# VectorE's SBUF-only steps and GpSimd's additions in turns, long-row copies of two weights in DRAM, and a new schedule table

## The chip, the core and the metric

The kernel runs on one core of a Trainium2 chip. The metric is the device time of one execution in microseconds. It is compared as the median of several runs; the kernel before has a median of 1410.25 us over 3 runs (1404.16 to 1413.4).

Five engines work side by side, each through its own queue of instructions in a fixed order: TensorE (PE, matrix products), ScalarE (ACT, here the exponentials), VectorE (DVE), GpSimd (POOL) and SyncE (SP, which issues transfers). They wait for each other by semaphores.

## The reference

Two transformer-like blocks are applied twice to x of 2048 rows and 512 columns, all in bfloat16:

```python
def _A_ref(x, wqkv, wo):                      # 32 heads of 16
    q, k, v = split(x @ wqkv)
    scores = einsum("bhqd,bhkd->bhqk", q, k) * (Dh ** -0.5)
    p = softmax(scores)
    return reshape(einsum("bhqk,bhkd->bhqd", p, v)) @ wo
def _B_ref(x, w1, w2):                        # 512 -> 1792 -> 512
    return maximum(x @ w1, 0) @ w2
x = x + _A_ref(_layernorm(x), wqkv, wo)
x = x + _B_ref(_layernorm(x), w1, w2)
x = x + _A_ref(_layernorm(x), wqkv, wo)
x = x + _B_ref(_layernorm(x), w1, w2)
```

Each attention has 32 x 2048 x 2048 scores, and each score needs an exponential. That is most of the work.

## The kernel before

**A planner writes the order.** The kernel's text is a planner: it keeps a clock for each engine (`now_pe`, `now_dve`, `now_pool`, `now_act`), adds a cost for every step it emits, and emits the next step that it believes to be ready. The result is a fixed order of instructions per engine. The costs are constants at the head (L78 to L91), such as `POOL_ADD`, the cost of one GpSimd addition, and `JOINING`, the cost of issuing one joining transfer (below). `STARTS`, `MORE`, `SLIP` and `RULES` (L96, L105) are tables of exceptions to the planner's rules, keyed by the number of the slot.

**Slots.** Scores are made in blocks of 128 keys by 512 queries. The main loop (L2066) takes three blocks in a turn, called a slot; there are 1365 slots. TensorE writes the three blocks into one of two PSUM tiles `ps_s` (L2231). ScalarE then takes the exponential of two or of all three of them in one instruction (L2249: 128x1024 or 128x1536).

**Pairs.** Where ScalarE takes two blocks, VectorE takes the third. Two such blocks, of two slots, make a *pair*. Their exponential is an approximation in integer words: VectorE turns the scores into 16-bit words (`first_step`, L1750: from PSUM to a buffer of `words`), GpSimd makes two shifted copies of the words with 64-bit integer additions (`shifted`, L1811: `up` and `down`, one instruction each for both blocks), and the copies enter the value product with weights. Where the keys have no copy of the values that is already scaled, VectorE scales `down` in place (`weigh`, L1816, SBUF to SBUF). Buffers for words are borrowed from whatever lies idle (x rows, weights, values), so the profile shows the same lines with many names.

**Joining.** Unjoined, a pair gives three products with the values. If the pair is *joined* (`joins`, L1795), GpSimd issues a transfer that adds the unshifted words onto `up` (`add`, L1829, 256 KB, done by the DMA engines), and two products are left. The issue is an instruction (DMA_DIRECT2D, L1830) in GpSimd's own queue, between its additions, and counts as busy time of GpSimd. In `chain` (L1800), the joining task is given a delay of 300 ns after its `up` (`late`), and an addition's result counts as made `BEHIND_IT` = 300 ns after the addition.

**Value products.** TensorE multiplies the exponentials and the words with the values (`pv`, L1404), four heads abreast, into `ps_o` or `ps_f`. Between scores and values it fits the other matrix products (L467, L707, L716): projections, output and the dense block.

**VectorE's other steps.** Most read PSUM. These read and write SBUF alone: `ln_apply` (L795, 60 times, the layer norm's second half), `weigh` (L1816), `scale_v` (L945, 12 times), `mul` (L1342, 43 times, the division by the softmax sum). Each stands in VectorE's queue where the planner put it.

**Weights.** W1 does not stay in SBUF. It streams through four buffers: `load_w1` (L1025) issues, on SP, one load for each 128 columns, straight from the input, four groups ahead; a row of such a load is 256 bytes. `w1_to_load` (L1064) loads ten more such pieces late in the run. `load_w2` (L1649) fetches pairs of 128-row pieces of w2 again after their place has served as words. `to_load` (L274) lists the first loads of wo and w2; from slot 30 on the main loop issues one a slot (L2299), the last six from slot 180 on.

Of the kernel before, what the change touches and what calls it, by code (L numbers as in the profile page):

```python
# [12 lines left out]
BF16 = mybir.dt.bfloat16  # L13
# [13 lines left out]
def kernel(  # L27
# [11 lines left out]
    P = 128  # L39
# [38 lines left out]
    POOL_ADD = 170.0 + 215.0 * GROUP  # L78
# [12 lines left out]
    JOINING, ADDED, BEHIND_IT = 870.0, 4300.0, 300.0  # L91
# [4 lines left out]
    STARTS, MORE, SLIP = {13: 0, 90: 1, 113: 1, 120: 1, 109: 1, 101: 1, 127: 1, 188: 1, 194: 1, 193: 0, 218: 1, 207: 0, 256: 0, 260: 0, 286: 1, 292: 0, 313: 0, 329: 1, 322: 1, 323: 0, 336: 1, 353: 0, 360: 0, 373: 0, 374: 0, 385: 0, 439: 0, 442: 1, 502: 1, 516: 0, 532: 0, 530: 0, 585: 1, 605: 0, 653: 0, 641: 0, 655: 0, 678: 1, 694: 0, 684: 0, 689: 1, 692: 0, 770: 0, 776: 1, 818: 1, 807: 1, 808: 0, 806: 0, 822: 0, 852: 1, 842: 0, 879: 0, 880: 0, 916: 0, 937: 0, 941: 1, 948: 0, 952: 1, 950: 1, 962: 1, 961: 0, 983: 0, 1015: 1, 1011: 1, 1003: 0, 1017: 1, 1021: 1, 1027: 1, 1026: 1, 1022: 1, 1056: 0, 1058: 1, 1044: 0, 1055: 0, 1076: 1, 1092: 0, 1108: 0, 1128: 1, 1139: 0, 1130: 1, 1131: 0, 1151: 1, 1150: 0, 1155: 0, 1146: 0, 1227: 0, 1235: 0, 1256: 1, 1285: 0, 1352: 0}, {18: 1.0, 12: 1.0, 87: 2.0, 107: 1.0, 103: -1.0, 119: 2.0, 126: 1.0, 158: 1.0, 181: 2.0, 201: 2.0, 233: -1.0, 238: 1.0, 240: 1.0, 242: 2.0, 245: 1.0, 258: 2.0, 264: 2.0, 265: -1.0, 266: 1.0, 300: 2.0, 308: 1.0, 320: 2.0, 318: -1.0, 348: 1.0, 361: -1.0, 395: -1.0, 412: 1.0, 401: 1.0, 402: 2.0, 422: 2.0, 426: 2.0, 439: 1.0, 441: -1.0, 452: -1.0, 453: 1.0, 465: 2.0, 500: -1.0, 507: 1.0, 515: 2.0, 531: 1.0, 536: -1.0, 533: 1.0, 560: 2.0, 574: 2.0, 580: 2.0, 575: -1.0, 589: -1.0, 631: -1.0, 645: -1.0, 666: -1.0, 675: -1.0, 680: 2.0, 767: 1.0, 762: 1.0, 770: 2.0, 813: 1.0, 811: 2.0, 802: 2.0, 827: 2.0, 855: -1.0, 841: 1.0, 847: 1.0, 868: -1.0, 874: -1.0, 878: 1.0, 884: -1.0, 908: -1.0, 927: 1.0, 942: 1.0, 945: -1.0, 959: 1.0, 965: 1.0, 997: -1.0, 1017: 2.0, 1046: 1.0, 1089: 1.0, 1100: -1.0, 1099: -1.0, 1158: -1.0, 1176: 2.0, 1234: 1.0, 1223: 1.0, 1222: 2.0, 1258: -1.0, 1326: -1.0, 1332: -1.0, 1331: -1.0, 1356: 2.0, 1347: 2.0, 1360: 2.0, 1362: 1.0, 1374: 1.0}, {88: -200.0, 133: -200.0, 175: -200.0, 184: -200.0, 227: 60.0, 367: 120.0, 366: 60.0, 364: 120.0, 418: 60.0, 401: 216.0, 415: 120.0, 445: 120.0, 451: 120.0, 459: 120.0, 463: 60.0, 482: 60.0, 519: 216.0, 518: 216.0, 515: 216.0, 549: 120.0, 572: 60.0, 574: 216.0, 568: 216.0, 592: 216.0, 589: 216.0, 594: 60.0, 621: 120.0, 652: 216.0, 646: 120.0, 642: 60.0, 663: -200.0, 697: 216.0, 682: 60.0, 754: 60.0, 746: 216.0, 742: -200.0, 771: 216.0, 817: 60.0, 809: 216.0, 802: 60.0, 850: -200.0, 848: 60.0, 859: 120.0, 909: 60.0, 916: 60.0, 902: 120.0, 935: -200.0, 974: 120.0, 992: -200.0, 996: 120.0, 1025: -200.0, 1064: 120.0, 1068: -200.0, 1097: 60.0, 1116: -200.0, 1169: 120.0, 1220: -200.0, 1218: 60.0, 1232: 216.0, 1234: -200.0, 1230: 60.0, 1256: 216.0, 1268: -200.0, 1264: 120.0, 1273: 120.0, 1332: 120.0, 1336: -200.0, 1340: 216.0, 1353: -200.0, 1347: 120.0, 1354: 120.0, 1376: 60.0}  # L96
# [8 lines left out]
    RULES = {1: {'young': 6, 'old': 4, 'slack': 1300.0, 'ahead': 1.0, 'haste': 1.3, 'fill': 4000.0, 'partial': 3, 'hold': 4}, 21: {'fill': 3000.0, 'join': 4000.0}, 81: {'cap': 3.0, 'hold': 2, 'join': 1500.0, 'over': 60.0, 'near': 6, 'far': 4, 'spare': 14, 'wide': 1}, 101: {'near': 8}, 121: {'near': 8, 'pressed': 2, 'soon': 1400.0, 'old': 4}, 141: {'wide': 0, 'closing': 9}, 161: {'pressed': 6, 'hold': 3, 'spare': 6, 'least': 0.8, 'far': 4, 'soon': 2000.0, 'haste': 1.6, 'near': 4}, 201: {'margin': 60.0, 'spare': 10, 'backlog': 2200.0, 'young': 6, 'far': 2, 'least': 0.5, 'hold': 2, 'slack': 1300.0}, 221: {'calm': 2.0, 'closing': 12, 'soon': 2000.0, 'pace': 1.3, 'partial': 2, 'cap': 10.0, 'keep': 1, 'young': 3}, 241: {'soon': 1400.0, 'slack': 1300.0, 'near': 8, 'most': 50.0, 'join': 5000.0, 'calm': 1.2, 'margin': 60.0, 'pace': 0.85}, 261: {'margin': 100.0}, 281: {'near': 14, 'spare': 20, 'join': 7000.0, 'pace': 1.3}, 301: {'late': 99.0, 'least': 0.5, 'unit': 400.0, 'easy': 1.0, 'keep': 2, 'young': 5, 'pace': 1.0, 'full': 3}, 321: {'spare': 10, 'keep': 3}, 361: {'least': 0.8, 'late': 99.0, 'soon': 2000.0, 'slack': 300.0}, 381: {'join': 5000.0, 'full': 2, 'easy': 1.2, 'closing': 6, 'hold': 2, 'cap': 3.0, 'unit': 400.0, 'fill': 3000.0}, 401: {'least': 1.0, 'calm': 9.0, 'keep': 2, 'ahead': 5.0, 'haste': 2.0, 'hold': 4, 'partial': 3, 'slack': 800.0}, 421: {'ahead': 12.0, 'pressed': 4}, 441: {'fill': 3000.0}, 461: {'partial': 3}, 481: {'share': 6, 'partial': 2}, 521: {'cap': 10.0, 'wide': 1}, 541: {'least': 1.0, 'spare': 10, 'young': 6, 'wide': 1}, 581: {'old': 5, 'far': 4}, 601: {'pace': 0.7, 'soon': 2000.0, 'least': 1.0, 'haste': 2.0}, 621: {'rounds': 4, 'calm': 3.0, 'near': 12, 'far': 3}, 641: {'ahead': 1.0}, 661: {'join': 4000.0, 'old': 4, 'share': 4, 'full': 3}, 681: {'closing': 3}, 741: {'over': 120.0, 'most': 50.0}, 761: {'room': 0, 'join': 5000.0}, 821: {'cap': 3.0, 'old': 5, 'share': 4, 'fill': 4000.0}, 841: {'backlog': 3000.0, 'fill': 3000.0}, 861: {'eager': 0}, 881: {'pace': 1.3}, 901: {'backlog': 3000.0, 'late': 99.0, 'soon': 1400.0, 'slack': 300.0, 'near': 10, 'fill': 2000.0, 'rounds': 3, 'pressed': 4}, 921: {'slack': 300.0, 'full': 3, 'share': 4, 'partial': 4, 'calm': 9.0, 'pressed': 6, 'easy': 1.0, 'least': 0.5}, 941: {'pace': 1.0, 'slack': 1300.0}, 961: {'unit': 320.0, 'margin': 100.0}, 981: {'spare': 10, 'least': 0.8, 'haste': 1.6, 'cap': 10.0, 'over': 120.0, 'keep': 2, 'ahead': 8.0, 'closing': 3}, 1021: {'least': 1.0, 'soon': 1000.0}, 1041: {'join': 4000.0, 'eager': 0}, 1081: {'spare': 20, 'haste': 1.3, 'over': 120.0, 'slack': 300.0, 'easy': 1.6, 'backlog': 1500.0, 'room': 0, 'pace': 0.85}, 1121: {'soon': 2000.0, 'haste': 1.6, 'hold': 2, 'easy': 1.6, 'share': 6, 'full': 5, 'backlog': 4000.0, 'calm': 1.0}, 1141: {'backlog': 3000.0}, 1161: {'hold': 3, 'old': 4, 'late': 3.0, 'over': 0.0}, 1221: {'least': 1.0, 'unit': 360.0}, 1241: {'share': 2, 'most': 50.0, 'late': 2.0, 'calm': 1.2, 'eager': 1, 'full': 4, 'hold': 3, 'margin': 100.0}, 1261: {'calm': 1.2, 'ahead': 3.0}, 1281: {'slack': 1300.0, 'spare': 14, 'eager': 0, 'calm': 1.0}, 1321: {'wide': 1, 'backlog': 1500.0, 'cap': 6.0, 'late': 2.0, 'least': 1.0, 'soon': 1400.0, 'slack': 1300.0, 'pressed': 6}, 1341: {'unit': 400.0, 'pressed': 4, 'far': 4, 'slack': 1300.0, 'pace': 0.7, 'ahead': 5.0, 'calm': 1.5, 'easy': 2.0}, 1361: {'partial': 4, 'margin': 200.0}}  # L105
# [36 lines left out]
    dram = ctx.enter_context(tc.tile_pool(name="dram", bufs=1, space=bass.MemoryType.DRAM))  # L142
    x_away = [dram.tile([P, 2, D], BF16, name=f"away{n}") for n in range(NTT // 2)]
# [130 lines left out]
    to_load = deque()  # L274
    for T in range(NDC):
        for e in range(2):
            rows = A_wo[T * P : (T + 1) * P, :].rearrange("(g e d) f -> e g d f", g=4, e=2)
            to_load.append((wo[1 - e : P : 2, T, :], rows[e]))
    for ft in range(NF):
        to_load.append((w2[:, ft, :], B_w2[ft * P : (ft + 1) * P, :]))  # L280

    make_identity(nc, ident[:])
    nc.gpsimd.memset(qbuf[1][:], 0.0)
    for k in range(2):
        load_w(nc.gpsimd, k, 1)
    ones = [vaug[0][kb] for kb in range(NKB)] + [vaug[1][kb] for kb in range(TPC)]

# [265 lines left out]
    def do_task(t):  # L553
# [16 lines left out]
        if t["engine"] == "pool" and "chain" in t:  # L570
            t["chain"]["issued"] += 1
            settle(t["chain"])

    def run_act():

        for t in act_q:
# [1919 lines left out]
```

## Time and profile before

| | |
|---|---|
| median of 3 runs | 1410.25 us |
| profiled execution, its time | 1409.86 us |
| its span, first to last instruction | 1408.0 us |
| granted TensorE clock, mean | 0.983 |
| ScalarE: first exponential starts, last ends | 11.1 us, 1385.8 us |
| GpSimd: first and last addition start | 40.9 us, 1379.0 us |

How to read it: "busy" is the time in which at least one instruction of an engine runs, so that instructions which overlap count once; the mean duration of a single instruction can be longer than the distance from one to the next, since the next is already taken in while the last one runs. Idle time of an engine is shown with what ended it. The 1.9 us between the span and the time of the execution lie before the first and after the last instruction.

### The profile page before, as it was taken

Reading aid. Unit: us, or ns where it says so; the run is one execution under the profiler, and the core shown is the slowest. Engines: PE = TensorE matmul, PEld = TensorE weight load, DVE = VectorE, ACT = ScalarE, POOL = GpSimd, SP = SyncE. Lnnn points to the kernel's source line nnn. Section 1 sums busy time; section 2 is a strip of 40 time slices with the busy share of each in tenths; the row PEclk is TensorE's granted clock in tenths of the full one; section 3 lists DMA queues with packets and bytes.
Section 4 is the critical chain, followed back from the end, with each engine's and each line's share of the span. In section 5 each row is a group of like instructions: output and inputs, shape, how many; then the busy total and the mean of one; then the engine's idle time right before and its main releaser. Section 6 shows DMA issues by size and latency. Waiting matters only on the chain.

```text
span 1408.0 us, 47339 instructions
## 1 busy us (share of the span) xinstructions
PE 1331.4 (95%) x19639; PEld 455.5 (32%) x19639; DVE 1208.0 (86%) x2055; ACT 1330.7 (95%) x1437; POOL 1194.0 (85%) x1800
## 2 busy tenths in 40 slices
PE   8899999998999999999899998999999999999988
PEld 3222222222222222222222222222234344445655
DVE  7998889888999889988798887998988788888774
ACT  8999999998999999999999998999999899999984
POOL 3687767999899999989699997889979799989781
PEclk9999999999999999999999999989999999999999
DMA  6761011887698697967678775669979888868782
GB/s 144 149 108 25 18 32 43 148 156 134 115 175 159 134 160 130 204 132 128 115 124 180 152 132 97 128 118 165 217 129 146 182 140 161 151 107 175 126 140 56
DMA packets 231143, 184.31 MB, mean 131 GB/s; under 512 B 144752, under 2 KB 168496, under 8 KB 230928
## 3 DMA queue, kind: packets, MB, share of 16 engines
q0 software_dynamic: 70368, 123.14, 52.1%
q1 hardware_dynamic: 159600, 57.70, 17.1%
q8 instruction: 153, 2.51, 0.8%
q10 hardware_dynamic: 960, 0.46, 0.1%
q14 instruction: 62, 0.51, 0.1%
HBM read 38.80 MB, written 4.19 MB: 31 GB/s over the span
## 4 chain that ended last, share of the span: by engine, by line
PE 38%; DVE 10%; ACT 9%; DMA 8%; POOL 7%; issue 4%; SPq 0%; DVEq 0%; POOLq 0%; ACTq 0%
PE ps_s L2231 14%; PE ps_f L1404 6%; PE ps_o L467 6%; ACT e L2249 6%; PE ps_o L1404 5%; PE ps_f L467 5%; POOL words L1811 3%; DVE words L1750 3%; DMA words<-words 2%; POOL words L1830 1%; ACT xx L2249 1%; DMA words<-xx 1%; DMA c<-r 1%; ACT w L2249 1%; DVE ot L1342 1%
## 5 line engine op out<-in xcount | busy, mean ns | idle before, releaser
L2249 ACT ACTIVATE e<-ps_s 128x1024 bf16<-128x1024 f32 (+1 forms) x775 | 821.5, 1146 | 28.3 <-PE ps_s L2231 25.9
L1750 DVE TENSOR_SCALAR words<-ps_s 128x512 int16<-128x512 f32 x838 | 561.8, 684 | 84.0 <-PE ps_s L2231 69.1
L2231 PE MATMUL ps_s<-q,ktp 32*128 32x512 bf16 (+2 forms) x4147 | 500.3, 335 | 23.5 <-ACT e L2249 7.9
L1811 POOL INT64_ADD words<-words x511 | 425.2, 956 | 77.2 <-DVE words L1750 70.0
L2231 PEld LDWEIGHTS <-ktp 32*128 32x128 bf16 x4429 | 154.5, 92 | 467.0 <-issue 459.1
L2249 ACT ACTIVATE xx<-ps_s 128x1024 bf16<-128x1024 f32 x202 | 217.4, 1089 | 10.4 <-PE ps_s L2231 10.2
L2231 PE MATMUL ps_s<-q,ktl 32*128 32x256 bf16 (+2 forms) x1368 | 205.3, 297 | 10.1 <-DVE words L1750 7.2
L1830 POOL DMA_DIRECT2D words<-words x187 | 198.7, 1063 | 2.5 <-POOL words L1811 0.9
L1404 PEld LDWEIGHTS <-vaug 128*32 128x32 bf16 x4244 | 112.5, 95 | 162.5 <-issue 146.6
L1404 PE MATMUL ps_o<-e,vaug 128*32 128x512 bf16 (+2 forms) x907 | 145.5, 351 | 0.5 <-DVE ht L1236 0.4
L1404 PE MATMUL ps_f<-e,vaug 128*32 128x512 bf16 (+2 forms) x834 | 126.5, 351 | 1.3 <-DVE q L977 0.6
L1750 DVE TENSOR_SCALAR xx<-ps_s 128x512 int16<-128x512 f32 x148 | 99.4, 684 | 18.7 <-PE ps_s L2231 14.1
L1811 POOL INT64_ADD xx<-words x106 | 99.7, 956 | 10.7 <-DVE words L1750 7.0
L2249 ACT ACTIVATE vaug<-ps_s 128x1024 bf16<-128x1024 f32 x90 | 95.0, 1077 | 3.5 <-PE ps_s L2231 3.3
L467 PE MATMUL ps_o<-w,ht 128*32 128x512 bf16 x1120 | 92.5, 383 | 2.2 <-DVE xn L996 1.1
L2231 PEld LDWEIGHTS <-ktl 32*128 32x128 bf16 x1368 | 64.0, 93 | 62.7 <-issue 61.2
L1404 PE MATMUL ps_o<-words,vaug 128*32 128x512 bf16 (+1 forms) x450 | 80.2, 354 | 3.1 <-DMA words<-words 2.4
L1404 PE MATMUL ps_o<-words,vscaled 128*32 128x512 bf16 (+2 forms) x482 | 80.8, 330 | 0.0
L1404 PEld LDWEIGHTS <-vscaled 128*32 128x32 bf16 x1576 | 68.3, 97 | 32.4 <-issue 25.6
L1811 POOL INT64_ADD words<-xx x87 | 75.9, 1009 | 3.2 <-PE ps_s L2231 0.9
L1404 PE MATMUL ps_f<-words,vaug 128*32 128x512 bf16 (+1 forms) x385 | 77.2, 374 | 0.1
L1404 PEld LDWEIGHTS <-val 128*32 128x32 bf16 x1968 | 60.7, 97 | 48.3 <-issue 39.9
(354 smaller groups left out, 3151.5 us busy)
## 6 DMA issues: line engine op xcount, KB each, us to landing
words<-words POOLq DMA_DIRECT2D x187, 256.0 KB, 4.1
w<-in_B_w_dram SPq DMA_DIRECT2D x144, 128.0 KB
xx<-words POOLq DMA_DIRECT2D x37, 256.0 KB, 4.2
w<-in_B_w_dram SPq DMA_DIRECT2D x35, 256.0 KB
words<-xx POOLq DMA_DIRECT2D x32, 256.0 KB, 4.6
w<-words POOLq DMA_DIRECT2D x27, 256.0 KB, 3.9
words<-w POOLq DMA_DIRECT2D x20, 256.0 KB, 3.9
words<-vaug POOLq DMA_DIRECT2D x12, 256.0 KB, 4.0
```

What stands on the lines that cost most here:

```text
L467: nc.tensor.matmul(G["b"][cols], lhsT[:, cols], rhs, start=not G["begun"][g], stop=not G["cols"][g], tile_position=(0, 32 * g), skip_group ...
L1342: nc.vector.tensor_mul(out=ot[T][:, at_column : at_column + width], in0=first[:, 0:width], in1=r[:, 0:width],)
L1404: nc.tensor.matmul((ps_f, ps_o)[sg["bank"]][32 * g : 32 * g + 32, 0 : sg["w"]], values[:, 4 * sg["T"] + g, 2 * e : 2 * e + 32], rhs, start ...
L1750: first = nc.vector.tensor_scalar(out=words[which][:, half * QS : (half + 1) * QS], in0=src, scalar1=EXP_BIAS, scalar2=THIRD, op0=ALU.add, ...
L1811: ins = nc.gpsimd.int64_add(of(part).bitcast(I64), of("lin").bitcast(I64), by)
L1830: ins = nc.gpsimd.dma_start(out=of("up").bitcast(BF16), in_=of("lin").bitcast(BF16), accum_op=ALU.add)
L2231: score = nc.tensor.matmul(b[:, a : a + sg["w"]], kt[32 * g : 32 * g + 32, kc : kc + P], q_home(sg["q"])[32 * g : 32 * g + 32, sg["e"], 0 ...
L2249: ex = nc.scalar.activation(out=eb[:, 0 : place[m]], in_=b[:, 0 : place[m]], func=ACTF.Exp, scale=1.0 / (LOG2E * UNIT),)
```

## The change

Four things are changed.

1. A flag `shared` marks the four kinds of VectorE steps that work from SBUF to SBUF. When the planner emits one, it first emits the GpSimd tasks that it believes can start before, and counts the VectorE step from where GpSimd's clock then stands. Then the next GpSimd *addition* gets a semaphore wait for that VectorE step, and GpSimd's clock is moved behind it plus 120 ns (`TURN`). Joining transfers get no such wait, and the VectorE steps themselves wait for nothing new.
2. Copies of W1 (14 pieces) and w2 (7 pieces) are written to DRAM, DRAM to DRAM, with one long row per partition: 1 KB for a piece of W1, 2 KB for a piece of w2. The loads of W1 after the first four, and the repeated loads of w2, read these copies. The W1 copies stand ahead of wo and w2 in `to_load`, the w2 copies behind.
3. The planner's costs change: `POOL_ADD` 600 to 590 ns (170 or 160 + 430), `JOINING` 870 to 620 ns, `ADDED` (from a joining's issue to its sum) 4300 to 4500 ns.
4. `STARTS`, `MORE`, `SLIP` and `RULES` have new entries throughout.

```diff
-    POOL_ADD = 170.0 + 215.0 * GROUP
+    POOL_ADD = 160.0 + 215.0 * GROUP
...
-    JOINING, ADDED, BEHIND_IT = 870.0, 4300.0, 300.0
+    JOINING, ADDED, BEHIND_IT, TURN = 620.0, 4500.0, 300.0, 120.0
...
-    STARTS, MORE, SLIP = {13: 0, 90: 1, ...
+    STARTS, MORE, SLIP = {73: 0, 76: 1, ...
...
-    RULES = {1: {'young': 6, 'old': 4, ...
+    RULES = {1: {'pressed': 2, 'rounds': 3, ...
...
+    w1_away = [dram.tile([P, NDC, P], BF16, name=f"w1_away{ft}") for ft in range(NF)]
+    w2_away = [dram.tile([P, 2, D], BF16, name=f"w2_away{n}") for n in range(NF // 2)]
...
-    to_load = deque()
+    def w1_of(ft):
+        return B_w1[:, ft * P : (ft + 1) * P].rearrange("(c p) f -> p c f", p=P)
+
+    to_load = deque((w1_away[ft][:], w1_of(ft)) for ft in range(NF))
...
+    for n in range(NF // 2):
+        to_load.append(
+            (
+                w2_away[n][:],
+                B_w2[2 * n * P : (2 * n + 2) * P, :].rearrange("(a p) f -> p a f", a=2),
+            )
+        )
...
             dve_q.remove(t)
-            dve_run(t["cost"], at(t["deps"], "dve"))
-        t["fn"]()
+            ready = at(t["deps"], "dve")
+            if t["shared"] and now_dve[0] > POOL_READY:
+                run_pool(max(now_dve[0], ready))
+                ready = max(ready, now_pool[0])
+            dve_run(t["cost"], ready)
+        given = t["fn"]()
+        if t["shared"] and now_dve[0] > POOL_READY:
+            turn[0] = given
+            now_pool[0] = max(now_pool[0], now_dve[0] + TURN)
...
+    def in_turn_pool(ins):
+        if turn[0] is not None:
+            tc.add_manual_dep(
+                ins.ins, turn[0].ins.name,
+                mybir.DependencyInfo(mybir.DependencyClass.Sync, mybir.DependencyReason.DATA),
[...]
+            )
+            turn[0] = None
+        return ins
...
-                in_=B_w1[:, ft * P : (ft + 1) * P].rearrange("(c p) f -> p c f", p=P),
+                in_=w1_away[ft][:] if n >= NW1 else w1_of(ft),
...
-                    out=home,
-                    in_=B_w1[:, of * P : (of + 1) * P].rearrange("(c p) f -> p c f", p=P),
+                    out=home, in_=w1_away[of][:],
...
-            in_=B_w2[2 * n * P : (2 * n + 2) * P, :].rearrange("(a p) f -> p a f", a=2),
+            in_=w2_away[n][:],
...
         def shifted(part, by):
-            ins = nc.gpsimd.int64_add(of(part).bitcast(I64), of("lin").bitcast(I64), by)
+            ins = in_turn_pool(
+                nc.gpsimd.int64_add(of(part).bitcast(I64), of("lin").bitcast(I64), by)
+            )
...
-            task(quick, weigh, [key + ("down",)], [key + first])
+            task(quick, weigh, [key + ("down",)], [key + first], shared=True)
...
-        if to_load and no >= (FIRST_LOAD if len(to_load) > NF - KEPT_Q else LATER_LOAD) and sp_free[0] < now_pe[0]:
+        if to_load and no >= (FIRST_LOAD if len(to_load) > NF + NF // 2 - KEPT_Q else LATER_LOAD) and sp_free[0] < now_pe[0]:
```

`ln_apply`, `scale_v` and `mul` get `shared=True` in the same way as `weigh`, and return their instruction.

More of the change, by code (lines that the diff above doesn't have):

```diff
@@ L410, with task @@
     hurry = [False]
-    def task(cost, fn, makes=(), deps=(), place=None, engine="dve"):
-        t = {"cost": cost, "fn": fn, "makes": makes, "deps": deps, "engine": engine}
+    def task(cost, fn, makes=(), deps=(), place=None, engine="dve", shared=False):
+        t = {
+            "cost": cost, "fn": fn, "makes": makes, "deps": deps, "engine": engine,
+            "shared": shared,
+        }
         q = {"dve": dve_q, "pool": pool_q, "act": act_q}[engine]
@@ L572, in do_task @@
             settle(t["chain"])
+    turn = [None]
+    def in_turn_pool(ins):
[3 more added lines that the diff above has]
+                mybir.DependencyInfo(mybir.DependencyClass.Sync, mybir.DependencyReason.DATA),
+                reason="the port to SBUF that both engines share",
+            )
+            turn[0] = None
+        return ins
     def run_act():
@@ L794, in ln_apply @@
         xn_waits[0] += i == TPC - 1
-        nc.vector.tensor_scalar(
+        return nc.vector.tensor_scalar(
             out=xnbuf[i][:], in0=x_t[tt][:],
@@ L840, in apply @@
             def apply(k):
-                ln_apply(tag, tt + k, k)
+                ins = ln_apply(tag, tt + k, k)
                 if not by_dma(tag):
-                    return
+                    return ins
                 home, a = (tag[2], 0) if tag[0] == "ln1" else columns(*tag[1:])[:2]
@@ L855, in apply @@
                     xn_free[0] = now_dve[0] + lag
+                return ins
             for k in range(n):
@@ L861, in ln_rows @@
                     [("xT", prev, k)] * (k < rows_of_prev) + [("rs", tag, 2)]
-                    + [("raw",)] * (k == TPC - 1 and ("raw",) in made),
+                    + [("raw",)] * (k == TPC - 1 and ("raw",) in made), shared=True,
                 )
@@ L947, in scale_v @@
             ),
-            [("third", l, kb)], [("v", l, kb)] + deps,
+            [("third", l, kb)], [("v", l, kb)] + deps, shared=True,
         )
@@ L1341, in mul @@
         def mul():
-            nc.vector.tensor_mul(
+            ins = nc.vector.tensor_mul(
                 out=ot[T][:, at_column : at_column + width], in0=first[:, 0:width],
@@ L1345, in mul @@
             )
+            return ins
         task(
@@ L1357, in finish_segment @@
             66 + 1.1 * width, mul, each(width // P, "ot", l, j, T) + [("m", n)],
-            [ready, ("both", n)] + war,
+            [ready, ("both", n)] + war, shared=True,
         )
@@ L1819, in weigh @@
             p["by"]["down"].append(ins)
+            return ins
         first = ("lower",) if not p["scaled"] else ("down",)
```

4 lines of the change are left out of this document (2 added, 2 removed).

## The prediction

> **What bounds the kernel now.** First the page's busy times. ScalarE and TensorE are both at 95%; GpSimd and VectorE look free.
>
> ```profile
> PE 1331.4 (95%) x19639; PEld 455.5 (32%) x19639; DVE 1208.0 (86%) x2055; ACT 1330.7 (95%) x1437; POOL 1194.0 (85%) x1800
> ```
>
> An average hides stages, so next the busy time by stretches. I cut the run into stretches of 70 slots at the starts of the exponentials (columns: stretch, its length, then PE, PEld, DVE, ACT and POOL busy, granted clock, DMA share, GB/s):
>
> ```profile
> 284.40:354.60 70.20, 66.00 (x778) 18.12 (x782) 60.52 (x97) 65.81 (x73) 69.83 (x105) 0.98 0.81 144
> 354.60:421.60 67.00, 65.38 (x811) 17.93 (x807) 63.06 (x107) 66.64 (x74) 61.81 (x93) 1.00 0.79 145
> 421.60:486.10 64.50, 64.50 (x833) 17.13 (x825) 57.48 (x91) 64.46 (x72) 64.04 (x98) 1.00 0.76 147
> 699.50:766.20 66.70, 63.72 (x731) 17.92 (x723) 62.44 (x102) 64.86 (x73) 65.15 (x98) 1.00 0.75 136
> 1130.90:1198.10 67.20, 65.89 (x1392) 29.01 (x1388) 58.20 (x101) 66.21 (x73) 66.27 (x99) 1.00 0.82 146
> ```
>
> In these stretches GpSimd is busy 98 to 99% (69.83 of 70.20, 64.04 of 64.50), once 92%. ScalarE's exponentials give the floor: the stretch at 421.6 has 70 two-block ones in 64.46 us, 0.92 us each. GpSimd stands right beside that floor.
>
> What one pair costs GpSimd, from its timeline (start, length):
>
> ```profile
> 430.42 1.18 POOL L1811 INT64_ADD val<-words  x1
> 431.01 1.17 POOL L1811 INT64_ADD words<-words  x1
> 431.60 1.17 POOL L1811 INT64_ADD wv<-words  x1
> ...
> 435.14 1.12 POOL L1830 DMA_DIRECT2D words<-words  x1
> 435.75 1.76 POOL L1811 INT64_ADD words<-words  x2
> 437.22 1.12 POOL L1830 DMA_DIRECT2D words<-words  x1
> ```
>
> Additions in a row start 0.59 us apart. Joining to joining, with a pair's two additions between, is 2.08 us, so a joining takes 2.08 - 1.18 = 0.90 us. That is the old planner constant (870 ns), not the new one (620).
>
> [...] VectorE's SBUF-only steps have a short form and a long tail (durations min/median/max in ns), while its PSUM reader L1750 has a mean of 684 and none above 702:
>
> ```profile
> L795 DVE TENSOR_SCALAR xn<-xx,mv,ya x60: 396/469/2228, 21.9 to 1390.9; 128x512 bf16<-128x512 bf16 x60
> L1816 DVE TENSOR_SCALAR words<-words x29: 403/542/2090, 43.3 to 1378.1; 128x1024 bf16<-128x1024 bf16 x29
> ```
>
> Over the shortest of each form, the 163 such steps lose 48.6 us. Against ScalarE's idle time between the exponentials (88 gaps over 0.1 us, 55.5 us together), sorted by what happened in the 2.2 us ahead of each: 23.5 us follow a step stretched by over 0.25 us, 15.2 a wait for a transfer, 2.7 both, 14.1 neither. [...]
>
> **The change part by part.** The two programs' instruction lists give the counts.
>
> *Exponentials.* 30 of 1365 slots change from two blocks on ScalarE to three (107 to 137), since 15 pairs fewer are made (629 to 614). A three-block one takes 1491 ns on average, a two-block one 1097 (rows by form): 30 x 0.394 = +11.8 us on ScalarE. VectorE loses 30 first steps x 0.684 = 20.5 us; it is not what ends, at 86%, and I take nothing for it (bounds 0 to the 14.1 us of unsorted gaps).
>
> *GpSimd.* 1258 to 1228 additions, but 450 to 490 joinings: -30 x 0.59 + 40 x 0.90 = +18.3 us in all, and unevenly spread. With 620 ns the planner believes a joined pair costs 1.18 + 0.62 = 1.80 us where the trace shows 2.08, and a pair comes at most every two slots, 1.84 us of ScalarE. So it joins nearly every pair in long rows. Load = pairs x 1.18 + joinings x 0.90, by slot (length, load and count before; after):
>
> | slots | length | before: pairs/joinings, load | after |
> |---|---|---|---|
> | 210 to 279 | 65.0 | 34/17, 55.4 | 34/35, 71.6 |
> | 280 | 70.2 | 34/28, 65.3 | 34/30, 67.1 |
> | 350 | 67.0 | 33/26, 62.3 | 33/32, 67.7 |
> | 420 | 64.5 | 35/22, 61.1 | 35/34, 71.9 |
> | 700 | 66.7 | 35/28, 66.5 | 34/34, 70.7 |
> | 770 | 67.7 | 34/26, 63.5 | 34/34, 70.7 |
> | 1120 | 67.2 | 33/25, 61.4 | 34/34, 70.7 |
> | sum | 468.3 | 435.5 | 490.4 |
>
> Measured GpSimd busy time in these seven is 445.0, 9.5 above the counted load (the 46 widening issues of L1326, 0.66 us, and edges). So after: 490.4 + 9.5 = 499.9 us of GpSimd work against 468.3 us now: +31.6. What hides a lag: a joined sum is first read a median of 11 slots (lowest tenth 8) after the slot of its second VectorE step, in both programs. At 0.956 us a slot (468.3/490) that is 10.5 (7.6) us, against 0.68 + 1.18 + 4.1 (issue to landing) = 6.0 us needed. Cover is 4.5, in the lowest tenth 1.6 us; I take 3, once for each of the three groups of neighbouring stretches: 31.6 - 9 = **+23 us**. Bounds: 0 (all hidden) and +31.6.
>
> *The rest of the run.* Of the 30 wide exponentials 6 fall into the seven stretches, 24 outside: 24 x 0.394 = **+9.5 us**. Outside, gaps behind stretched steps are 20.8 us (24.8 of other kinds). There the new wait helps: 112 additions carry it, so that the marked addition can't overtake a VectorE step. [...] I take half, **-10 us** (bounds 0 and -20.8). Inside the seven GpSimd has a backlog, the marked addition comes late anyway, and I take nothing.
>
> *The wait itself.* Behind a marked addition all of GpSimd's queue waits, joinings too, and TensorE's value products wait for both. Where GpSimd is late, the VectorE step is long done: 0. Where VectorE is late, up to about the step and one ahead of it, 0.40 + 0.68 = 1.1 us, 112 times. I take 0 by the backlog.
>
> *Order.* 115 of the 490 joinings (none of 450 before) stand behind the next pair's first addition: 0.59 us later, within the cover.
>
> *TensorE.* 206 value and projection matmuls less, 156 score matmuls more (repeats into spare time); at 0.39 us, four and three abreast, 20 us each way: 0.
>
> *Layout and SP.* A W1 load turns from 512 packets of 256 B into 128 of 1 KB, a w2 load from 256 to 128. One gap is due to W1 (1.4 us at 1276). W1's packets hold under half of the 17.1% of q1; 40 more joinings add 40/450 of 52.1% to q0, 4.6 points. They pull against each other: 0 (bounds: -15.2, the gaps behind transfers, and +1.4, that share's growth of 9% of them). SP issues 21 more transfers at 0.4 to 0.7 us; wo moves back 14 places in its queue, from 49 to 62 us, and is first read at 197.9; w2 at 279.5, its last first load issued at 196.5 with the copies behind it. Cover over 80 us.
>
> Sum on the profiled execution: 1409.9 + 23 + 9.5 - 10 = 1432.4. It lies 0.4 us from the median, so **1433 us**.
>
> **The rivals.**
> - *The turns don't work*: where GpSimd lags, unmarked additions starve VectorE as before. No relief: 1409.9 + 23 + 11.8 = 1445. For it: only 112 of 1228 additions are marked, VectorE waits for nothing. Chance 0.24.
> - *The turns stall GpSimd*: some 40 of the 112 (490/1365) lie in the seven stretches; at 1.1 us they add 44 to GpSimd there: 1433 + 44 = 1477. It decides if VectorE is later than GpSimd; the waits of L1811 for L1750 (91 us, 76 times) speak for it, the 98% against. Chance 0.08.
> - *GpSimd's lag is hidden*, because the reading order has more slack than its first readers show: 1409.9 + 11.8 - 10 = 1412. Chance 0.14. One form of it: issuing a joining costs GpSimd next to nothing, so that 34 joined pairs load it with 40 us; the 2.08 us period speaks against it, and it has 0.02 of the 0.14. [...]
> - *Faster*: the lag is hidden and all gaps behind stretched steps go, with half of those behind transfers: 1409.9 + 11.8 - 26.2 - 7.6 = 1388. It decides at the cost of a joining: at 0.62 us instead of 0.90, a stretch of 34 joined pairs loads GpSimd with 61 us, below the 64.4 us of ScalarE. Against it is the same timeline. Chance 0.14.
>
> **How the numbers follow.** The forecast has 0.40, at 1433 with its own range of 1415 to 1446 (cover from 5 to 0 us a group, relief from all to a quarter). The range of 1403 to 1462 leaves out most of the faster case and the stalled one. About 1%, 14 us, can be told from no change. Slower by more: 0.40 + 0.24 + 0.08 less 0.05 for the forecast's lower edge = 0.67; within: 0.14 + 0.05 = 0.19; faster 0.14.
>
> **What would show it.** Right: GpSimd at 97% or more in slots 210 to 490, 700 to 840 and 1120 to 1190, these stretches at 70 us and over, TensorE's waits naming GpSimd's words or landings of joinings, SBUF-only steps seldom above 1 us, joinings still 0.90 us. Wrong: joinings at 0.62 us, or those stretches at 66 us with GpSimd full and no waits (hidden); the stall rival shows as GpSimd idle behind L795 or L1816.

## The result: 3% slower

| | before | after |
|---|---|---|
| median of 4 runs each | 1409.06 us | 1452.76 us (1440.81 to 1457.28) |
| ratio, 95% interval | | 1.0298 [1.0224, 1.0372] |
| profiled execution, its span | 1408.0 us | 1455.5 us |
| ScalarE busy | 1330.7 us | 1346.8 us |
| ScalarE's gaps over 0.1 us between exponentials | 55.5 us | 86.0 us |
| granted TensorE clock | 0.983 | 0.970 |

The profiled execution of after is the longest of its four, 4.5 us over the median. From the first exponential to the last it takes 47.1 us more than before: 16.1 is ScalarE's own work, the rest its idle time, nearly all of it in the gaps of the table.

From the page of after: the busy times, the two large DMA queues, and the chain of work that ended last.

```profile
PE 1353.8 (93%) x19589; PEld 465.0 (32%) x19589; DVE 1167.1 (80%) x2023; ACT 1346.8 (93%) x1437; POOL 1207.5 (83%) x1810
...
q0 software_dynamic: 76128, 133.63, 54.3%
q1 hardware_dynamic: 112192, 61.43, 16.4%
...
PE 28%; POOL 17%; ACT 11%; DMA 7%; issue 5%; DVE 4%; POOLq 0%; DVEq 0%; SPq 0%; ACTq 0%
```

GpSimd's share of the whole span went down, from 85% to 83%. In the chain its share went up: before, the same line reads

```profile
PE 38%; DVE 10%; ACT 9%; DMA 8%; POOL 7%; issue 4%; SPq 0%; DVEq 0%; POOLq 0%; ACTq 0%
```

VectorE's 10% have become 4%, GpSimd's 7% have become 17%. The stretches of 70 slots show where. First four of the seven in the prediction's table (slots 280, 350, 770, 1120), then four outside it (slots 490, 840, 1190, 1260), in after; the columns are those of the prediction:

```profile
292.40:363.00 70.60, 66.18 (x761) 17.84 (x764) 57.72 (x95) 66.40 (x73) 70.60 (x105) 1.00 0.84 150
363.00:437.30 74.30, 69.37 (x804) 18.93 (x800) 63.35 (x107) 67.49 (x74) 70.67 (x106) 0.98 0.83 146
801.40:876.50 75.10, 69.25 (x845) 17.71 (x843) 55.47 (x88) 66.77 (x72) 72.82 (x107) 0.95 0.86 167
1165.60:1231.80 66.20, 64.64 (x1333) 28.26 (x1329) 56.12 (x99) 65.91 (x73) 65.81 (x98) 1.00 0.89 157
...
509.40:586.40 77.00, 68.68 (x760) 20.19 (x756) 58.68 (x104) 69.37 (x75) 67.41 (x101) 0.96 0.81 141
876.50:945.70 69.20, 66.10 (x777) 19.21 (x771) 62.88 (x110) 68.87 (x73) 48.91 (x77) 1.00 0.38 73
1231.80:1307.60 75.80, 69.88 (x1508) 32.14 (x1500) 58.88 (x104) 68.00 (x73) 75.11 (x111) 0.95 0.88 173
1307.60:1388.80 81.20, 74.00 (x2025) 45.23 (x2021) 58.58 (x117) 70.55 (x73) 65.72 (x97) 0.85 0.77 139
```

Slots 770, 840 and 1190 in before (280, 350 and 1120 stand in the prediction):

```profile
766.20:833.90 67.70, 66.14 (x830) 17.55 (x833) 56.48 (x90) 65.01 (x71) 62.55 (x95) 0.97 0.79 157
833.90:910.90 77.00, 70.50 (x773) 20.23 (x766) 66.73 (x110) 71.91 (x73) 61.88 (x88) 0.96 0.64 117
1198.10:1267.10 69.00, 66.32 (x1436) 30.62 (x1430) 59.83 (x104) 65.31 (x73) 64.75 (x99) 0.98 0.72 131
```

The seven stretches went from 468.3 to 498.4 us, with GpSimd busy 95 to 100% of each. They did not grow alike: by -1.0 us (slot 1120, where ScalarE is busy for 65.91 of 66.20) to +7.6 (slot 420). Outside them the run grew by 17.0 us, in both directions: at slot 840 the joinings issued within the stretch fell from 29 to 13, GpSimd stands at 48.91 of 69.20 us and the stretch is 7.8 us shorter; at slot 1190 they rose from 22 to 29, GpSimd stands at 75.11 of 75.80 and the stretch is 6.8 longer. Slots 490 and 1260 grew as much, by 6.6 and 6.2 us, but there GpSimd is not full (67.41 of 77.00 and 65.72 of 81.20): at 490 a single landing holds TensorE for 5.2 us (below), and at 1260 the clock is at one half for 23.9 us; what led to that is not shown.

The cost of a joining has not changed. GpSimd's timeline of after (start, length):

```profile
439.92 1.18 POOL L1848 INT64_ADD words<-words  x1
440.50 1.17 POOL L1848 INT64_ADD ktl<-words  x1
441.39 1.12 POOL L1869 DMA_DIRECT2D words<-words  x1
441.99 1.76 POOL L1848 INT64_ADD words<-words  x2
443.47 1.12 POOL L1869 DMA_DIRECT2D words<-words  x1
```

Joining to joining with two additions between is 443.47 - 441.39 = 2.08 us, as before: 0.90 each, not 0.62.

What TensorE waits for (in all, times, longest), in after:

```profile
PE ps_s L2270 <- ACT e L2288: 10.6, 38, 0.7
PE ps_s L2270 <- DVE words L1786: 7.5, 8, 2.0
PE ps_f L1440 <- DMA words<-words: 5.6, 6, 1.7
PE ps_f L1440 <- DMA words<-xx: 5.3, 4, 2.0
PE ps_f L1440 <- DMA val<-words: 5.2, 1, 5.2
PE ps_o L1440 <- DMA words<-words: 4.5, 5, 1.6
...
PE ps_f L1440 <- POOL words L1848: 3.3, 8, 0.7
```

and in before:

```profile
PE ps_s L2231 <- DVE words L1750: 12.7, 13, 2.7
PE ps_s L2231 <- ACT e L2249: 11.4, 49, 0.6
PE ps_o L1404 <- DMA words<-words: 3.1, 4, 1.3
```

Summed over all lines, TensorE's waits for VectorE fell from 39.2 to 21.7 us, those for landings (in after nearly all of joinings) rose from 8.4 to 32.0, those for GpSimd from 0.4 to 11.4. What VectorE no longer delays, GpSimd and the joinings do, for longer.

One such stall shows what follows it. The chain of work around slot 730 in after, in order of time (start, length, what):

```profile
756.20 1.51 POOL words L1848 x2
757.71 1.12 POOL words L1869
758.83 0.80 POOL words L1848
759.62 0.59 POOL w L1848
760.21 0.04 issue
760.26 0.56 PE ps_o L1440 x4
760.82 0.54 PE ps_s L2270 x3
761.36 0.54 PE ps_o L1440 x3
```

and the stretches around it (length, busy times, granted clock, share of the DMA engines, GB/s):

```profile
757.40:760.40 3.00, 1.37 (x16) 0.49 (x13) 3.00 (x5) 2.48 (x3) 3.00 (x6) 0.99 0.95 163
760.40:763.80 3.40, 3.40 (x22) 0.56 (x19) 2.15 (x4) 1.91 (x2) 3.40 (x7) 0.50 1.15 167
763.80:767.20 3.40, 3.37 (x26) 0.59 (x22) 1.90 (x3) 2.80 (x4) 3.40 (x7) 0.50 1.10 173
767.20:770.60 3.40, 3.40 (x25) 0.58 (x22) 2.46 (x5) 2.79 (x4) 2.51 (x5) 0.50 0.63 111
770.60:774.00 3.40, 3.40 (x43) 0.99 (x40) 2.68 (x5) 3.35 (x4) 2.86 (x5) 1.00 0.29 51
```

TensorE waits for GpSimd's queue: two additions, a joining, two more additions. The idle time before its next product is 1.44 us. Then its clock is granted at one half for 10.2 us: 22 to 26 matmuls in 3.4 us instead of 43, and ScalarE is busy for 7.5 of these 10.2 us. In the 3 us with the stall ScalarE was idle for 0.5 us; in the 10.2 us behind it, for 2.7.

### The profile page after: what moved, and what is told of

The parts are those of the page before. It is cut to its first block, busy times and chain, and to the rows that moved or that the text cites. A ratio compares the mean times of both kernels' runs of the same rounds, so it can differ in the third digit from the quotient of the medians.

```text
span 1455.5 us, 47267 instructions
## 1 busy us (share of the span) xinstructions
PE 1353.8 (93%) x19589; PEld 465.0 (32%) x19589; DVE 1167.1 (80%) x2023; ACT 1346.8 (93%) x1437; POOL 1207.5 (83%) x1810
## 4 chain that ended last, share of the span: by engine, by line
PE 28%; POOL 17%; ACT 11%; DMA 7%; issue 5%; DVE 4%; POOLq 0%; DVEq 0%; SPq 0%; ACTq 0%
PE ps_s L2270 10%; POOL words L1848 8%; ACT e L2288 5%; PE ps_f L1440 5%; PE ps_o L1440 4%; POOL words L1869 4%; PE ps_o L483 3%; PE ps_f L483 3%; DMA words<-words 3%; ACT xx L2288 2%; ACT w L2288 2%; POOL xx L1848 2%; DVE words L1786 2%; DMA xx<-vaug 1%; POOL w L1848 1%
## 5 line engine op out<-in xcount | busy, mean ns | idle before, releaser
L2288 ACT ACTIVATE e<-ps_s 128x1024 bf16<-128x1024 f32 (+1 forms) x574 | 653.1, 1196 | 44.2 <-PE ps_s L2270 42.6
L1786 DVE TENSOR_SCALAR words<-ps_s 128x512 int16<-128x512 f32 x872 | 585.8, 684 | 134.6 <-PE ps_s L2270 103.7
L1848 POOL INT64_ADD words<-words x575 | 531.1, 1131 | 102.9 <-DVE words L1786 75.4
L1869 POOL DMA_DIRECT2D words<-words x227 | 289.3, 1319 | 3.0 <-POOL words L1848 1.9
L2288 ACT ACTIVATE xx<-ps_s 128x1024 bf16<-128x1024 f32 x262 | 277.6, 1099 | 12.2 <-PE ps_s L2270 9.7
L2288 ACT ACTIVATE w<-ps_s 128x1024 bf16<-128x1024 f32 x106 | 113.1, 1103 | 9.6 <-PE ps_s L2270 9.6
L1440 PE MATMUL ps_o<-e,vaug 128*32 128x512 bf16 (+2 forms) x694 | 114.6, 346 | 0.3 <-DVE ht L1271 0.3
L2288 ACT ACTIVATE wv<-ps_s 128x1024 bf16<-128x1024 f32 x84 | 90.5, 1087 | 4.5 <-PE ps_s L2270 4.1
L1440 PE MATMUL ps_f<-words,vscaled 128*32 128x512 bf16 (+2 forms) x550 | 83.3, 334 | 3.2 <-POOL words L1848 3.0
L2288 ACT ACTIVATE val<-ps_s 128x1024 bf16<-128x1024 f32 x74 | 81.2, 1110 | 2.5 <-PE ps_s L2270 2.2
```

Source lines behind the costliest of these rows:

```text
L1440: nc.tensor.matmul((ps_f, ps_o)[sg["bank"]][32 * g : 32 * g + 32, 0 : sg["w"]], values[:, 4 * sg["T"] + g, 2 * e : 2 * e + 32], rhs, start ...
L1786: first = nc.vector.tensor_scalar(out=words[which][:, half * QS : (half + 1) * QS], in0=src, scalar1=EXP_BIAS, scalar2=THIRD, op0=ALU.add, ...
L1848: nc.gpsimd.int64_add(of(part).bitcast(I64), of("lin").bitcast(I64), by)
L1869: ins = nc.gpsimd.dma_start(out=of("up").bitcast(BF16), in_=of("lin").bitcast(BF16), accum_op=ALU.add)
L2288: ex = nc.scalar.activation(out=eb[:, 0 : place[m]], in_=b[:, 0 : place[m]], func=ACTF.Exp, scale=1.0 / (LOG2E * UNIT),)
```

## The experiments

Ratios are to the kernel before on the same chip, with their 95% intervals. "Excess" is, as in the prediction, what VectorE's SBUF-only steps take over the shortest of their form (48.6 us before, 21.6 after).

### The turns alone, both ways

**a_nowait**: the changed kernel, every order kept, the semaphore waits left away.

```diff
     def in_turn_pool(ins):
-        if turn[0] is not None:
+        if False:
             tc.add_manual_dep(
```

> The changed kernel, every engine's order unchanged, without the 112 waits of additions for VectorE's SBUF-only steps. Theory (GpSimd has too many joinings to issue, and that costs the time): the load stays, GpSimd is again 95 to 100% busy in slots 210 to 490; the stretched VectorE steps come back (over 40 us lost in them instead of some 20) and with them 5 to 18 us: 1455 to 1470 us. Rival (the waits themselves stall GpSimd): without them 1415 to 1430 us.

Measured 1449.55 us, 1.0303 [1.0274, 1.0332]: the same as after. The waits do act in the trace. The layer norm's step (min/median/max in ns), first without and then with them:

```profile
L830 DVE TENSOR_SCALAR xn<-xx,mv,ya x60: 396/448/1635, 20.7 to 1430.8; 128x512 bf16<-128x512 bf16 x60
```

```profile
L830 DVE TENSOR_SCALAR xn<-xx,mv,ya x60: 395/410/1157, 20.9 to 1438.0; 128x512 bf16<-128x512 bf16 x60
```

The excess goes from 36.8 to 21.6 us with the waits. But in this order they neither cost nor gain a measurable time; the result lies between what the two theories expected, and bears out neither size. Two things more can be read from this run. The changed order alone brings the excess from 48.6 down to 36.8 us. And its seven stretches take 498.9 us, those of after 498.4, although its clock is at one half for 47.7 us and not for 88.5: the loss is there with no more time at half clock than before has (47.6).

**b_turns**: the kernel before, every order kept, only the waits added (`shared=True` on the four steps and `in_turn_pool` around the addition, as in the change; no cost, table or load changed).

```diff
-            ins = nc.gpsimd.int64_add(of(part).bitcast(I64), of("lin").bitcast(I64), by)
+            ins = in_turn_pool(
+                nc.gpsimd.int64_add(of(part).bitcast(I64), of("lin").bitcast(I64), by)
+            )
...
-            task(quick, weigh, [key + ("down",)], [key + first])
+            task(quick, weigh, [key + ("down",)], [key + first], shared=True)
```

> The kernel before, every engine's order unchanged, with the waits alone added: the next addition after each SBUF-only VectorE step waits for it. Theory (the waits are a gain, the schedule is the loss): the steps lose under half of the 48.6 us, ratio 0.985 to 0.995, 1390 to 1403 us. Rival (the waits stall GpSimd): ratio 1.01 or more, GpSimd idle behind L795, L1816, L1342.

Measured 1394.65 us, 0.9912 [0.9882, 0.9943]: faster, by about 12 us. The excess fell from 48.6 to 14.6 us, ScalarE's gaps behind stretched steps from 23.5 to under 2 us (those behind transfers nearly doubled). The layer norm's step:

```profile
L809 DVE TENSOR_SCALAR xn<-xx,mv,ya x60: 396/406/1209, 21.7 to 1380.0; 128x512 bf16<-128x512 bf16 x60
```

The seven stretches take 467.9 us, 0.4 less than before; outside them the run is 10.2 us shorter. So the turns work and pay on the order of before, outside its full stretches, as the prediction had them. The loss lies in the rest of the change. That GpSimd's work stretches these steps is shown here: only the waits of its additions were added, and the excess fell by 34.0 us. What holds a step up in the chip is not shown. The expectations below call this loss the stalls at the port.

### The cost of a joining in the planner

**b_join620** and **b_join900**: the kernel before with one constant changed. 900 is a control: the tables of exceptions were made for 870, and any other cost makes them fit less.

```diff
-    JOINING, ADDED, BEHIND_IT = 870.0, 4300.0, 300.0
+    JOINING, ADDED, BEHIND_IT = 620.0, 4300.0, 300.0     # or 900.0
```

> The kernel before with one number changed: the planner's cost of a joining is 620 ns and not 870, so it plans 537 joinings and not 450 (1254 additions and not 1258). No waits, no copies, the tables of before. Theory (that cost makes the loss of the change): GpSimd's work rises by 87 x 0.91 = 79 us, GpSimd is 97 to 100% busy over long rows of slots, TensorE waits for landings and words: ratio 1.02 to 1.05. Rival (the new tables make the loss, the cost does not matter): ratio 0.99 to 1.01.

> The kernel before with that cost at 900 ns: 445 joinings, 1236 additions, 129 three-block exponentials and not 107. It shows what any new plan under the old tables does. ScalarE +22 x 0.39 = 8.7 us, GpSimd -18 us. Theory: ratio 1.00 to 1.01. If a plan that differs at all loses much here (the tables fit one plan only): ratio 1.02 or more, and the run with 620 ns proves less.

Measured 1487.39 us, 1.0567 [1.0522, 1.0611] at 620 (537 joinings), and 1431.83 us, 1.0163 [1.0117, 1.021] at 900 (445 joinings). Both are slower than I expected. The control costs some 23 us by itself, presumably since the tables no longer fit its plan. The 56 us between the two are beyond that. At 620 TensorE's waits for landings are 46.2 us.

**a_join900**: the changed kernel, its tables, loads and waits, with the measured cost.

```diff
-    JOINING, ADDED, BEHIND_IT, TURN = 620.0, 4500.0, 300.0, 120.0
+    JOINING, ADDED, BEHIND_IT, TURN = 900.0, 4500.0, 300.0, 120.0
```

> The changed kernel with the planner's cost of a joining at 900 ns, about what the trace shows: 392 joinings and not 490, 1192 additions, 173 three-block exponentials and not 137. ScalarE has 36 x 0.39 = 14 us more than the changed kernel, GpSimd 110 us less. Theory: the waits for landings and words go, the new tables no longer fit the plan (about 13 us): ratio to before 1.00 to 1.02, 1409 to 1437 us. Rival (cost is not the cause): 1.03 or more.

Measured 1407.1 us, 0.9994 [0.9964, 1.0024]. One constant takes back the whole loss, although 36 more exponentials are wide (173 against 137) and the tables were made for 620. 392 joinings are left of 490. TensorE's waits for landings fall from 32.0 to 6.0 us, those for GpSimd from 11.4 to 0.2. Its stretches at slots 280 and 770:

```profile
285.50:352.60 67.10, 64.86 (x790) 19.00 (x788) 54.26 (x92) 67.06 (x74) 61.34 (x96) 1.00 0.70 130
...
765.90:833.10 67.20, 66.64 (x852) 18.71 (x846) 52.65 (x83) 67.20 (x71) 61.35 (x92) 1.00 0.75 150
```

GpSimd stands at 61 of 67 us, and ScalarE is never idle in either (67.06 of 67.10, 67.20 of 67.20); the seven together take 472.6 us. This constant moves the whole plan, so the run shows that the joinings' believed cost carries the loss, not by which path.

**a_oldtables**: the changed code with the tables and costs of before.

```diff
-    POOL_ADD = 160.0 + 215.0 * GROUP
+    POOL_ADD = 170.0 + 215.0 * GROUP
...
-    JOINING, ADDED, BEHIND_IT, TURN = 620.0, 4500.0, 300.0, 120.0
+    JOINING, ADDED, BEHIND_IT, TURN = 870.0, 4300.0, 300.0, 120.0
...
-    STARTS, MORE, SLIP = {73: 0, 76: 1, ...
+    STARTS, MORE, SLIP = {13: 0, 90: 1, ...
...
-    RULES = {1: {'pressed': 2, 'rounds': 3, ...
+    RULES = {1: {'young': 6, 'old': 4, ...
```

> The changed kernel with the tables and the costs of before: the waits and the planner's turns, the long rows, 416 joinings, 1206 additions, 159 three-block exponentials. ScalarE +52 x 0.39 = 20 us against before, stalls at the port -15 us, tables that don't fit +13 us: ratio 1.00 to 1.02. Rival (the planner's turns are a gain by themselves): below 0.991, less than the kernel before with the waits alone.

Measured 1407.64 us, 1.0011 [0.9985, 1.0038]: no change from before. The new code replans even with the old costs (416 joinings, 159 wide exponentials). ScalarE's gaps fall to 32.6 us, but it is busy for 1346.7 us and not 1330.7: the 52 more wide exponentials take up most of what the gaps gave back.

### How a joining costs: GpSimd's time, or the landing

**a_half_cols** and **a_half_rows**: the changed kernel, every order kept, each joining cut to half its bytes, either to 512 of 1024 columns or to 64 of 128 rows.

```diff
-                out=of("up").bitcast(BF16), in_=of("lin").bitcast(BF16), accum_op=ALU.add
+                out=of("up").bitcast(BF16)[:, 0:QS], in_=of("lin").bitcast(BF16)[:, 0:QS], accum_op=ALU.add
```

and `[0:64]` in both places for the rows.

> The changed kernel with every joining transfer cut to the first 512 of its 1024 columns in all 128 partitions (the other half of the sums is left out): half the bytes, the same number of rows. Theory (the issue on GpSimd is the load): an issue still takes about 0.9 us, GpSimd stays full in slots 210 to 490, at most 10 us gained by earlier landings: 1440 to 1453 us. Rival (the landings wait behind too many bytes on the DMA engines): landing falls by 0.5 us or more and the time to 1415 to 1430 us.

> The changed kernel with every joining transfer cut to 64 of its 128 partitions (the other half of the sums is left out): half the bytes, half the rows. Theory: the issue falls towards the 0.6 to 0.66 us of the widening issues, which have 64 rows as well; GpSimd has 490 x 0.25 = 120 us less work and falls to some 90% in slots 210 to 490: 1412 to 1430 us, well below the run with half the columns. Rival (bytes on the DMA engines): the same time as the run with half the columns.

| | after | half the columns | half the rows |
|---|---|---|---|
| time, us | 1452.76 | 1420.23 | 1411.07 |
| ratio to before | 1.0298 [1.0224, 1.0372] | 1.0096 [1.0081, 1.0111] | 1.003 [1.0015, 1.0045] |
| addition's end to issue's end, median | 0.833 us | 0.833 us | 0.782 us |
| issue's end to landing, median | 3.16 us | 2.02 us | 2.58 us |
| the seven stretches | 498.4 us | 486.0 us | 481.2 us |
| TensorE waits for landings, for GpSimd | 32.0, 11.4 us | 12.6, 20.2 us | 17.2, 11.3 us |

Two of the stretches with half the columns (slots 280 and 350), and its costliest joinings (KB each, median us from issue to landing):

```profile
289.80:361.00 71.20, 66.20 (x760) 17.75 (x759) 57.75 (x95) 66.53 (x73) 71.20 (x105) 1.00 0.53 91
361.00:432.20 71.20, 67.68 (x804) 18.76 (x800) 63.83 (x107) 67.22 (x74) 70.38 (x105) 1.00 0.56 99
```

```profile
words<-words POOLq DMA_DIRECT2D x227, 128.0 KB, 3.5
```

My theory was that the issue's time on GpSimd is the cost; half the columns, which leave that time as it is, were to give back 10 us at most. They gave back some 28 (2.0% by the ratios), with landings 1.1 us sooner: what the rival had expected. GpSimd is even fuller than in after (71.20 of 71.20 us; 482.7 of 486.0 over the seven stretches), so its backlog alone does not make the 44 us: of the 30 us by which the seven grew it leaves some 18. Half the rows cut the issue by 0.05 us (I had expected about 0.25) and gained 9 us more, although their landing is later than with half the columns: GpSimd's time counts as well. What TensorE waits for is a path, the pair's place in GpSimd's queue plus the landing. Either part shortens it. The share of the DMA engines' time (the last column but one) fell as well, at slots 280 and 350 from 0.84 and 0.83 to 0.53 and 0.56; how much of the landing's 3.16 us is waiting for busy DMA engines, these runs do not separate.

**a_no_join** and **b_no_join**: both kernels without any joining, all other instructions in their order; the unshifted words of the joined pairs don't enter the values, and no third product takes their place.

```diff
-            ins = nc.gpsimd.dma_start(
-                out=of("up").bitcast(BF16), in_=of("lin").bitcast(BF16), accum_op=ALU.add
-            )
-            p["by"]["up"].append(ins)
```

> The changed kernel with no joining issued at all (the unshifted words of 490 pairs are left out of the output); TensorE, VectorE and ScalarE keep their orders. Theory (the joinings make the whole loss): GpSimd's work falls by 490 x 0.91 = 446 us, landings can't be late, only the 11.8 us of ScalarE and the old head and tail stay: 1380 to 1395 us. Rival (the new order of TensorE and ScalarE is worse by itself): 1405 us or more.

> The kernel before with no joining issued (the unshifted words of 450 pairs are left out of the output), all other orders kept. Theory: the 15 us of gaps behind transfers fall to 5 or so, the stalls at the port stay in part, since additions follow each other less: 1385 to 1398 us; the changed kernel without joinings stands within 10 us of it, where with them it is 44 us slower.

Measured 1352.77 us, 0.9606 [0.9562, 0.965], and 1347.71 us, 0.9574 [0.9529, 0.9619]: both fell much further than expected. After without joinings, its busy times, and a wait of ScalarE for TensorE (in all, times, longest):

```profile
PE 1299.8 (96%) x19587; PEld 458.8 (34%) x19589; DVE 1151.4 (85%) x2023; ACT 1329.5 (98%) x1437; POOL 777.4 (58%) x1320
```

```profile
ACT e L2284 <- PE ps_s L2266: 0.7, 2, 0.5
```

In after, with joinings, the same wait is

```profile
ACT e L2288 <- PE ps_s L2270: 42.6, 46, 4.7
```

Without joinings ScalarE's gaps are 1.9 us (after) and 4.7 us (before) in the whole run: it alone sets the end. Between the two kernels 5.1 us are left (the wide exponentials: ScalarE busy 1329.5 against 1320.6 us). So of the 43.7 us between the medians, 38.6 arise only where joinings are issued. By the ratios they cost the kernel before 4.3% (some 60 us) and the changed one 6.9% (some 97 us), against kernels that leave the sums out.

### The layout in DRAM

**a_direct**: the changed kernel, all loads from the inputs (the copies are still written).

```diff
-                in_=w1_away[ft][:] if n >= NW1 else w1_of(ft),
+                in_=w1_of(ft),
...
-                    out=home, in_=w1_away[of][:],
+                    out=home, in_=w1_of(of),
...
-            in_=w2_away[n][:],
+            in_=B_w2[2 * n * P : (2 * n + 2) * P, :].rearrange("(a p) f -> p a f", a=2),
```

> The changed kernel, which still makes its copies of W1 and w2 in DRAM, but with every load from the inputs as before (256-byte rows of W1). TensorE, VectorE, ScalarE and GpSimd keep their orders. Theory: the loads are four groups ahead and no part of the loss: within 5 us of the changed kernel, ratio to before 1.026 to 1.036. Rival (long rows shorten the joinings' landings, since they share the DMA engines): 10 us or more slower, landings 0.2 us later.

Measured 1450.79 us, 1.0293 [1.0248, 1.0337]: the long rows are worth nothing that can be measured here.

**b_turns_rows**: b_turns with the copies and the loads from them, TensorE's, VectorE's and GpSimd's orders unchanged; the loads' edits are those of the change itself.

```diff
+    w1_away = [dram.tile([P, NDC, P], BF16, name=f"w1_away{ft}") for ft in range(NF)]
+    w2_away = [dram.tile([P, 2, D], BF16, name=f"w2_away{n}") for n in range(NF // 2)]
...
-                    in_=B_w1[:, of * P : (of + 1) * P].rearrange("(c p) f -> p c f", p=P),
+                    in_=w1_away[of][:],
```

> The kernel before with the waits and with the long-row copies, the orders of TensorE, VectorE and GpSimd unchanged. Theory: the copies add little to the gain of the waits alone (0.9912): 0.987 to 0.993, 1388 to 1397 us. Rival: rows matter, 0.98 or less.

Measured 1391.36 us, 0.9884 [0.9834, 0.9935]. It beats both kernels, by 18 us and by some 60. What the rows add to b_turns (1394.65) lies inside both intervals. ScalarE's largest wait, where before has 25.9 us:

```profile
ACT e L2274 <- PE ps_s L2256: 16.1, 25, 1.9
```

## Why the prediction was right, and where it was short

The direction, the mechanism of the loss and the range held, but the range of 1403 to 1462 was wide: two of the rivals' times, 1412 and 1445, lie in it. The time of 1433 us was 20 us short, and the measured one lies above the forecast's own range of 1415 to 1446. On the profiled executions the change is +47.4 us against the +22.5 of the sum. The two terms that were off make up nearly all of the difference: the seven stretches by 7.1 us, the relief outside by 18.5. By its steps:

- *What a joining costs, and what a plan with 620 ns does.* Right. Joinings still take 0.90 us, nearly every pair is joined in the seven stretches (226 joinings and 233 pairs issued there), GpSimd is full there, and the whole cost goes away with the constant (a_join900).
- *+23 us in the seven stretches.* Measured +30.1, of which ScalarE's idle time is 22.6 and its own work 7.5. They take 498.4 us where I counted 499.9 us of GpSimd's work, but that they agree is in part chance: GpSimd was busy for 486.2 us of them, since some of the counted work ran in the slots behind, and idle for the rest. Nor was it all alike: of the signs that I had named, five of the seven stretches reached 70 us (slots 700 and 1120 did not) and five reached 97% (350 and 420 did not), and slot 1120, with 70.7 us of counted load, even got shorter. In the sum the cover of 3 us a group was too much. I had reckoned it against a landing of 4.1 us after the issue's start; in after a tenth of the joinings land more than 4.8 us after its end, and one, at slot 490, 8.3 us after its start (the stall of 5.2 us in the list of waits). a_half_cols shows how much hangs on the landing: the same GpSimd work, landed 1.1 us sooner, and the seven stretches take 486.0.
- *+9.5 us for wide exponentials outside.* Right: ScalarE's work outside grew by 8.6.
- *-10 us of relief outside.* This step failed: that half of the 20.8 us would go was my estimate, with no run behind it, and ScalarE's idle time outside grew by 8.5 us. At slots 840 and 910 it did fall, from 9.1 to 1.0 us, but not by the turns: without their waits (a_nowait) it is 2.7, so most of the fall is the new order's, with 29 joinings down to 13 at slot 840. And slots 490, 1190 and 1260, which my list of full stretches left out, grew by 6.6, 6.8 and 6.2 us; ScalarE's idle time in these three rose from 12.5 to 26.1 us. Without joinings (a_no_join) it is 1.0 there. b_turns shows that the size was sound for the order of before (10.2 us outside the seven stretches); a_nowait, that in the changed order it is nothing that can be measured.
- *The waits, the layout.* Nothing each, as taken: a_nowait and a_direct. TensorE's waits for words and landings, which should have told of the lag, did.
- *A term that the sum did not have: the clock.* After has 88.5 us at half the TensorE clock, before 47.6. Of ScalarE's gaps 38.1 us lie in these times or within 1 us behind them, against 18.3: 19.8 of the 30.5 us by which the gaps grew. The prediction priced a stall at its own length. But a_nowait has no more time at half clock than before and loses the same 3% (though some 6 us more of its gaps lie behind stretched steps), so it is not shown that the clock makes any of the loss: the gaps may be the stalls' own. No run held the clock fixed.

The worst of the stretched steps of before stands in neither of the prediction's two lines: a division lost 2.27 us (L1342, 128x512, 2943 ns against 675 for the shortest), the layer norm's worst 1.83 (2228 against 396). No term of the sum used either.

The rivals: *the turns don't work* gave 1445, nearer to the time than my 1433. Its mechanism, steps starved as before, the traces refute: the excess fell from 48.6 to 21.6 us, 15.2 of it by the waits (though the longest division, L1377, still takes 1.61 us). Its price, no relief, is what a_nowait measured. *The turns stall GpSimd*: GpSimd is idle behind those steps for 38.0 us in all, and taking the waits away gains nothing. *The lag is hidden* and *faster* fell with the stretches; that joinings are cheap to issue is refuted by the 2.08 us.

Left open: why single landings take 8 us; what part of the loss is GpSimd's time, the landing, or the clock, since the halved joinings change all three; and whether tables made for the true cost, with the turns, would beat 1391 us; this was not tried.

## What to carry to other kernels

A cost constant in a planner is a claim about the chip: read it off the timeline (here 2.08 - 1.18 us) before tuning tables around it, because one that is too low can fill an engine whose average looks harmless (83% here). For an asynchronous step count the whole path, its place in the issuing queue plus the landing with its late tail, against when the result is first read. Judge a synchronisation on the order it was meant for: the same semaphores gained 12 us on one plan and nothing on another.

## What the hardware showed that was not expected

- **TensorE's clock fell to one half behind stalls of mostly 1 to 3 us, each time for longer than the stall.** In after the clock dropped to 0.50 in 13 periods behind the start, 3.4, 6.8, 10.2 and once 23.9 us long, each behind a gap in TensorE's work or within it; before it was 11 periods. Not every stall has one: of the 21 gaps of 1 us and over in after, 14 end less than 3 us ahead of a drop or stand across its start, and of the 11 of 1.5 us and over, 10. For 12 of the 13 periods the longest gap was 1.0 to 3.2 us (1.44 at 760 us), only once more (5.2). Without joinings (a_no_join) there was no drop before the last 3 us, and the granted clock was 1.000.
- **The issue of an accumulating transfer cost GpSimd nearly the same in all three sizes**: 0.833 us with 256 and with 128 KB of 128 rows, 0.782 with 128 KB of 64 rows. The landing came sooner with half the bytes, but not by the bytes alone: 3.16, 2.02 and 2.58 us after the issue's end.
- **A row's length in DRAM did not show in the time**: 256 bytes or 1 KB for W1, 1450.79 and 1452.76 us.
